# Attention and two dense stages on one core: batches one by one, the first weights kept in SBUF, W13 first, and a front in a fixed order on every engine

## The chip, the cores and the metric

The kernel runs on one core of one Trainium2 chip. The metric is the device time of one execution in microseconds (us). Matrix products run on TensorE (PE in the profile; PEld is its weight load), elementwise work on VectorE (DVE), ScalarE (ACT) and GpSimd (POOL). SyncE (SP) issues nearly all transfers.

## What is computed

```
pp  = softmax(scale * p k^T) v            # p: 32 packed queries a head; 8 batches, 8 heads, 576 keys, 64 wide
x   = softmax(scale * q pp^T) pp          # 576 queries a batch, over the 32 packed rows
x2  = ((x w1) * (x w2)) w3 w_out          # 4608 tokens, 512 -> 1024 -> 1024 -> 512
out = leaky(x2 w_in) w_out2               # 512 -> 2048 -> 512, leaky is max(0.01 h, h)
```

The inputs q, k, v and p are float32. The six weights are 64-bit floats, read as pairs of 32-bit words and turned into float32 on the chip.

## The kernel before

**The two phases.** Phase A makes x2, batch by batch, and stores it in HBM (`x2d`). Phase B makes the last line of the reference from it with a seven-product scheme (`sevens`, `h_unit`, `o_unit`). The diff changes how phase A is ordered; of phase B only where its preparation is called.

**The products.** An fp32 operand is split into a rounded high part and the rest (`hi` by ACT, `lo` by a subtraction on DVE or POOL), and `three` makes each product in three passes: hi hi, hi lo, lo hi. A pass loads 128x128 weights and streams the columns of one tile. The small attention products and M run in plain float32 on parts of the array, in bundles of eight matmuls (`eights`).

**A batch of phase A.** `s1` (scores of p on k), `e` (exp), `n` (sum and reciprocal), `t` (transposes), `y` (times v) give the packed rows `ppT`. `S`, `E`, `N`, `X` give the attention weights AT, split in two. Since x is AT times the packed rows, the kernel multiplies the packed rows by w1|w2 first: M = ppT (w1|w2), eight units `m_mm`/`m_split` of 256 columns for each of the two halves of the heads. Then a = M1 AT and b = M2 AT: 16 units of 12 passes of 288 columns (`ab_unit`), each of which copies a on ACT, multiplies it with b on DVE (line 463) and splits the product. Last, x2 is (a*b) W13 with W13 = w3 w_out, 8 units of 24 passes (`x2_unit`). W13 itself is made once, in 384 passes of 256 columns (`w13_half`).

**The order.** Batches go in pairs. For a pair all ab units come first (`ab_stage`), then all x2 units (`x2_stage`), with the attention of the next pair spread beside them. One set of split ab tiles fits in SBUF, so the second batch's a*b (and part of batch 0's) is stored to HBM (`abd`, line 96) and read back (`reload_ab`). The converted w1|w2 is stored too (`w12d`), and read back for each later pair (`load_w`). The front, a written `SCRIPT`, holds the attention of batches 0 to 3, the ab units of batches 0 and 1, and W13 at its end. The instructions are emitted in that order, and the framework's scheduler may still move them on each engine.

**A conversion of a weight block** (128x512 pairs, 512 KB): ACT makes the low word (line 296), DVE the high bits in two instructions (lines 298 and 302), POOL adds the two (line 305). There are 16 blocks of w3, 8 of w_out and 16 of w1|w2 in the front, and 32 of phase B's weights later (`pump`). For W13 the word is also split: `hi` on ACT, `lo` on DVE or POOL.

Of the kernel before, what the change touches and what calls it, by code (L numbers as in the profile page):

```python
# [10 lines left out]
SCRIPT = """k0 p0 k1 lw0 v0 s0 v1 cw0 e0 q0 n0 s1 q1 t0 e1 lw1 n1 y0 t1 p1 k2 dw0 y1 S0 cw1 k3 v2 E0 S1 s2 v3 dw1 lw2 N0 E1 e2 q2 X0 N1 n2 s3 t2 q3 X1 e3 cw2 lw3 n3 y2 t3 dw2 M00 lw4 a00 y3 S2 cw3 lw5 S3 dw3 Z M01 a01 A000 E2 cw4 lw6 A001 dw4 cw5 E3 dw5 M02 a02 A100 N2 lw7 A101 cw6 x2 M10 a10 A200 N3 dw6 cw7 A201 x3 lw8 dw7 M03 a03 A010 cw8 lw9 A011 dw8 lo0 M11 a11 A300 cw9 lw10 A301 dw9 co0 M04 a04 A110 cw10 lw11 A111 dw10 do0 M12 a12 A400 cw11 lw12 A401 dw11 lo1 O0 M05 a05 A210 cw12 lw13 A211 dw12 co1 M13 a13 A500 cw13 lw14 A501 dw13 lo2 do1 M06 a06 A310 cw14 lw15 A311 dw14 O1 co2 M14 a14 A600 cw15 lo3 A601 dw15 do2 co3 M07 a07 A410 O2 lo4 do3 A411 co4 lo5 M15 a15 A700 O3 l30 do4 A701 co5 lo6 c30 M16 a16 A510 o4 l31 do5 d30 A511 co6 c31 o5 M17 a17 A610 p2 lo7 do6 d31 A611 o6 l33 co7 l35 A710 H0 h1 do7 c33 p3 A711 o7 k4 d33 c35 l32 H3 d35 l37 c32 H5 d32 l34 c37 H2 k5 d37 c34 l38 k6 l315 d34 H4 h7 s4 c38 d38 W00 l36 c36 l39 l310 d36 h6 c39 l311 H8 e4 l312 W01 t4 W10 W20 s5 c311 v4 k7 d39 l313 d311 c310 c312 e5 c313 d310 h9 W30 v5 d312 H11 W21 h10 s6 l314 W11 n4 c314 d313 d314 q4 v7 W31 y4 t5 W40 s7 H12 q5 W41 h13 W50 n5 e6 v6 c315 d315 n6 H14 t6 W51 y5 e7 H15 y6 W60 n7 W61 W70 W71"""  # L11
KQ = {"k": 1}
# [15 lines left out]

# [4 lines left out]
def tile_kernel(ctx, tc, qT, kT, vL, pT, w12, w3b, wo1, win, wo2, out):  # L33
# [29 lines left out]
    def ps_pv():
        return ps_tile([P, 512], "pv", 2) if psum["early"] else ps_at()[:, 0]
# [5 lines left out]

    stA = ExitStack()
    main = stA.enter_context(tc.tile_pool(name="main", bufs=1, side="right"))
    stT = ExitStack()
# [3 lines left out]
    w12d = dram.tile([16, P, 512], F32, name="w12d")  # L79
    wid = dram.tile([16, P, 512], F32, name="wid")  # L80
    wod = dram.tile([16, P, 512], F32, name="wod")
    abd = dram.tile([B, 8, P, S], F32, name="abd")
    pks = [att.tile([P, 4, 32], F32, name=f"pks{i}") for i in range(2)]
    ppT = [att.tile([P, 4, 32], F32, name=f"ppT{i}") for i in range(4)]

    later = []
    RAW, VB, C64, C32, WSP, AB32, CT = 4, 5, 3, 6, 4, 7, 5

    def store(out, in_):

        later.append((out, in_))

    def stores(keep=0):
        while len(later) > keep:
            o, i = later.pop(0)
            nc.scalar.dma_start(out=o, in_=i)
# [8 lines left out]
    fence, float32s = [], []  # L105

    def together(ins, begin=False):

        if begin:
            del float32s[:]  # L110
        if float32s:
            after(ins, float32s[-1])
        else:
            tc.keep_in_program_order(ins)
        float32s.append(ins)
        fence[:] = [ins]

    def three(dst, lhs, rhs, first=True, last=True):

        for n, (i, j) in enumerate(PASSES):  # L120
            ins = nc.tensor.matmul(dst, lhs(i), rhs(j), start=first and n == 0, stop=last and n == 2)  # L121
            if fence:
                after(ins, fence.pop())
# [5 lines left out]
    s1q, s2q = {}, {}  # L129
    raws, vs, s1p, Ps, PTs, s2p, ATs = {}, {}, {}, {}, {}, {}, {}  # L130

    def half_tile(th):
        return main.tile([P, 2, TH], F32R, tag=f"ab{th}", name="ab", bufs=8)

    kq_tag = dict(KQ)

    def held(b, ins):

        if b in (2, 3):
            tc.keep_in_program_order(ins)  # L140

    def load_kq(key, b, g):
        for j in range(2):
            if key in kq_tag and b < 2:
                t = rd(half_tile(kq_tag[key])).rearrange("p a s -> p (a s)")
            else:
                t = att.tile([P, S], F32, tag="raw", name="raw", bufs=RAW)
            held(b, nc.sync.dma_start(out=t, in_=(kT if key == "k" else qT)[b, 2 * g + j]))
            raws[key, b, g, j] = t

    def spare_v(b, g):

        if (b, g) != (0, 1):
            return None
        t = main.tile([P, 2, S], F32, tag="AT", name="v", bufs=4)
        return t.rearrange("p a s -> p (a s)")[:, :5 * P].rearrange("p (c d) -> p c d", c=5)

    def load_v(b, g):
        for j in range(2):
            t = spare_v(b, g) if psum["early"] else None  # L160
            if t is None:
                t = att.tile([P, 5, P], F32, tag="v", name="v", bufs=VB)
            src = vL[b, 2 * g + j]
            held(b, nc.sync.dma_start(out=t[:, 0:4], in_=src[0:512].rearrange("(p c) d -> p c d", c=4)))
# [45 lines left out]
    def s1_norm(b, g):  # L210
        _, st = s1p[b, g]
# [41 lines left out]
    def s2_mm(b, g):
        if g == 0:
            s2q[b] = scores(ppT[b % 4], "q", b, b)
        ps = s2q[b][g]
        t = att.tile([P, 18, 32], F32, tag="sT", name="sT", bufs=2)
        nc.vector.transpose(out=t.rearrange("p (a n) c -> p a (n c)", a=2), in_=ps[:, :, :TH])
# [3 lines left out]
        s2p[b, g] = t, st  # L262

    def s2_exp(b, g):
        t, _ = s2p[b, g]
        nc.scalar.activation(out=t, in_=t, func=AF.Exp, scale=SCALE)

    def s2_norm(b, g):
        t, st = s2p[b, g]
# [6 lines left out]
        s2p[b, g] = a32  # L276

    def s2_split(b, g, engine=nc.vector):
        a32 = s2p.pop((b, g))
        at = main.tile([P, 2, S], F32R, tag="AT", name="AT", bufs=4)  # L280
        nc.scalar.copy(at[:, 0], a32)
        sub(engine, at[:, 1], a32, at[:, 0])
        ATs[b, g] = at


    def conv(dst, d, in_turn=lambda ins: None):
# [3 lines left out]

        hw, lw = d[:, :, 1], d[:, :, 0]
        q = dst.bitcast(I32)
        t = att.tile([P, 512], U32, tag="cT", name="cT", bufs=CT)
        in_turn(nc.scalar.activation(out=q, in_=lw, func=AF.Copy, scale=2.0 ** -29))
        in_turn(
            nc.vector.tensor_scalar(  # L298
# [730 lines left out]
```

## Time and profile before

| what | value |
|---|---|
| median of 3 runs | 1357.84 us (1357.84 to 1358.12) |
| profiled execution, its own time | 1356.27 us |
| its span, first to last instruction | 1354.3 us |
| PE busy | 1286.0 us, 95% |
| DVE, ACT, POOL busy | 894.1 us (66%), 629.3 us (46%), 115.7 us (9%) |
| moved by DMA | 323.62 MB |
| DMA issues to and from `abd` | 80 and 80, 144 KB each |
| DMA issues to and from `w12d` | 16 of 256 KB and 24 of 512 KB |

The profiled execution took 1.97 us more than its span, and the median is 1.57 us above it. A busy PE is not a PE at its peak, so the passes are counted in the rows below, and not its share alone.

### The profile page before, as it was taken

How to read it: one execution, taken by the hardware profiler on the slowest of the kernel's cores; microseconds unless marked ns; L12 is line 12 of the kernel's file. 1: busy time of each engine (PE TensorE's matmuls, PEld its weight loads, DVE VectorE, ACT ScalarE, POOL GpSimd, SP SyncE). 2: the span in 40 equal slices, each digit the busy share in tenths (PEclk: the TensorE clock that was granted, in tenths of full speed). 3: DMA queues.
4: the chain of work that ended last, by engine and by line, in shares of the span. 5: the costliest groups of instructions: out<-in, count | busy, mean ns of one | idle time of the engine just before them, and what ended most of it. 6: DMA issues, size and time to landing. Idle time of an engine off the chain costs nothing.

```text
span 1354.3 us, 25514 instructions
## 1 busy us (share of the span) xinstructions
PE 1286.0 (95%) x9752; PEld 1207.4 (89%) x9752; DVE 894.1 (66%) x1514; ACT 629.3 (46%) x1213; POOL 115.7 (9%) x94
## 2 busy tenths in 40 slices
PE   4587899999999999999999999999999999999998
PEld 1476798989988897899999999999999999999998
DVE  3869647765876595572977665847665468596667
ACT  2445344454455544453665555545434344354432
POOL 1245421211001200000000000000000000000000
PEclk9999999999999999999999999999999999999999
DMA  9578769768986873297878976467546754778884
GB/s 319 175 235 267 262 200 286 240 215 267 316 282 213 279 249 124 71 310 250 300 267 291 316 262 234 163 215 246 185 142 214 235 184 167 258 272 305 281 307 152
DMA packets 171258, 323.62 MB, mean 239 GB/s; under 512 B 18048, under 2 KB 89728, under 8 KB 171136
## 3 DMA queue, kind: packets, MB, share of 16 engines
q1 hardware_dynamic: 150400, 300.74, 66.1%
q10 hardware_dynamic: 20736, 21.24, 4.6%
q8 instruction: 77, 1.26, 0.4%
q14 instruction: 45, 0.37, 0.1%
HBM read 226.75 MB, written 95.16 MB: 238 GB/s over the span
## 4 chain that ended last, share of the span: by engine, by line
PE 77%; DMA 12%; DVE 7%; issue 2%; ACT 1%; SPq 1%; ACTq 0%; POOL 0%; DVEq 0%; POOLq 0%
PE mm L121 26%; PE b L884 26%; PE c L884 13%; PE a L884 6%; PE at L177 3%; DMA xh<-xfd 3%; DMA c<-w 2%; DMA xl<-xfd 1%; DVE cT L298 1%; DMA part<-o 1%; DVE cT L302 1%; DMA c<-w3b 1%; PE at L238 1%; DMA v<-vL 1%; DMA wi<-wid 1%
## 5 line engine op out<-in xcount | busy, mean ns | idle before, releaser
L121 PEld LDWEIGHTS mm<-AT,M 128*128 128x128 f32 x1536 | 210.8, 191 | 44.8 <-issue 17.1
L121 PE MATMUL mm<-AT,M 128*128 128x288 f32 x1536 | 231.2, 304 | 15.2 <-DVE ab L463 8.9
L884 PE MATMUL b<-xh,wi 128*128 128x384 f32 x768 | 219.0, 338 | 5.7 <-DMA xh<-xfd 3.7
L884 PE MATMUL b<-gh,wo 128*128 128x384 f32 x768 | 213.9, 335 | 1.4 <-DVE o L847 1.4
L121 PE MATMUL mm<-ab,W 128*128 128x288 f32 x1536 | 208.0, 295 | 0.0
L121 PEld LDWEIGHTS mm<-ab,W 128*128 128x128 f32 x1536 | 203.7, 188 | 4.5 <-issue 1.8
L884 PEld LDWEIGHTS b<-xh,wi 128*128 128x128 f32 x768 | 141.5, 189 | 8.0 <-DMA xh<-xfd 2.9
L884 PEld LDWEIGHTS b<-gh,wo 128*128 128x128 f32 x768 | 140.2, 188 | 2.3 <-issue 1.0
L884 PE MATMUL b<-xl,wi 128*128 128x384 f32 x384 | 129.2, 337 | 0.1
L884 PE MATMUL b<-gl,wo 128*128 128x384 f32 x384 | 128.4, 334 | 0.0
L884 PE MATMUL c<-xh,wi 128*128 128x384 f32 x384 | 106.1, 335 | 1.9 <-DMA xh<-xfd 1.9
L884 PE MATMUL c<-gh,wo 128*128 128x384 f32 x384 | 107.2, 335 | 0.6 <-DVE o L842 0.5
L658 ACT CAST gh<-gr 128x1152 fp32r<-128x1152 f32 (+1 forms) x72 | 75.6, 1051 | 68.8 <-PE b L884 32.5
L126 DVE TENSOR_TENSOR gl<-gr,gh 128x1152 fp32r<-128x1152 f32 (+1 forms) x72 | 87.7, 1223 | 23.9 <-ACT gh L658 23.9
L305 POOL TENSOR_TENSOR c<-cT,c 128x512 int32<-128x512 int32 x56 | 76.0, 1358 | 301.6 <-DVE cT L302 102.6
L126 DVE TENSOR_TENSOR ab<-ab,ab 128x288 fp32r<-128x288 f32 x128 | 57.8, 479 | 46.6 <-ACT ab L442 46.2
L658 ACT CAST gh<-gs 128x1152 fp32r<-128x1152 f32 (+1 forms) x54 | 56.9, 1054 | 64.0 <-PE b L884 34.8
L463 DVE TENSOR_TENSOR ab<-mm,a 128x288 f32<-128x288 f32 x128 | 57.8, 454 | 36.3 <-PE mm L121 24.6
L832 ACT ACTIVATE gr<-gr 128x1152 f32<-128x1152 f32 (+1 forms) x54 | 57.3, 1062 | 46.2 <-DVE gr L847 45.9
L884 PEld LDWEIGHTS b<-xl,wi 128*128 128x128 f32 x384 | 72.6, 189 | 0.7 <-DMA xl<-xfd 0.7
L884 PEld LDWEIGHTS c<-xh,wi 128*128 128x128 f32 x384 | 69.9, 188 | 2.9 <-DMA xh<-xfd 2.0
L884 PEld LDWEIGHTS b<-gl,wo 128*128 128x128 f32 x384 | 72.1, 188 | 0.2 <-DVE gl L126 0.2
(135 smaller groups left out, 2092.2 us busy)
## 6 DMA issues: line engine op xcount, KB each, us to landing
xh<-xfd SPq DMA_DIRECT2D x126, 384.0 KB, 5.7
xl<-xfd SPq DMA_DIRECT2D x126, 384.0 KB, 5.4
part<-o SPq DMA_DIRECT2D x48, 384.0 KB, 2.8
o<-part SPq DMA_DIRECT2D x48, 384.0 KB, 4.0
c<-wo SPq DMA_DIRECT2D x24, 512.0 KB, 4.6
w<-w12d SPq DMA_DIRECT2D x24, 512.0 KB, 4.2
abd<-ab ACTq DMA_DIRECT2D x80, 144.0 KB, 3.5
ab<-abd SPq DMA_DIRECT2D x80, 144.0 KB, 4.1
```

Source lines behind the costliest of these rows:

```text
L121: ins = nc.tensor.matmul(dst, lhs(i), rhs(j), start=first and n == 0, stop=last and n == 2)
L126: engine.tensor_tensor(out=out, in0=x, in1=rd(hi), op=ALU.subtract)
L177: ins = nc.tensor.matmul(dst(h)[c * 32:c * 32 + 32], lhs[r, c, :], rhs(c)[r], start=True, stop=True)
L238: ins = nc.tensor.matmul(ps[r, :64], PT[:K, c, r], v[:K, c, g * 64:g * 64 + 64], start=c == 0, stop=c == 4)
L298: nc.vector.tensor_scalar(out=t, in0=hw, scalar1=3, scalar2=0x3FFFFFFF, op0=ALU.logical_shift_left, op1=ALU.bitwise_and)
L302: nc.vector.scalar_tensor_tensor(out=t, in0=hw, scalar=0xC0000000, in1=t, op0=ALU.bitwise_and, op1=ALU.bitwise_or)
L305: return lambda: nc.gpsimd.tensor_tensor(out=q, in0=t.bitcast(I32), in1=q, op=ALU.add)
L463: nc.vector.tensor_tensor(out=t, in0=pb[:, :TH], in1=a, op=ALU.mult)
L658: nc.scalar.copy(hi[step], x[step])
L832: nc.scalar.activation(out=out, in_=x, func=AF.Prelu, alpha=0.01)
L884: nc.tensor.matmul(dst, lhs(l), rhs(r), start=first and n == 0, stop=last and n == total - 1, skip_group_check=True)
```

## The change

- One batch after the other: 16 ab units, then the 8 x2 units, with the attention of the next batch spread beside them (`pieces`, `slots`, `attention`). a*b is never stored. `abd` and `w12d` are gone.
- w1|w2 stays in SBUF as float32 in four tiles of 2048 columns (`ring`), in the buffers that the split w3 used before. M is made in four units of 512 columns a batch instead of eight of 256, in two PSUM banks each; its tiles have two buffers instead of three.
- W13 is made first, in 192 passes of 512 columns, with four accumulation banks open at a time. The front holds attention and all other work of batch 0, and attention of batch 1.
- The front's steps are finer (one engine each), and `manual_schedule` keeps every engine in the script's order.
- Seven buffers take weight blocks in the front (three, and four halves of the unused M tiles). The loop converts phase B's blocks as before.
- Phase B's preparation (`make_wi(0)`) comes 9 units into the last batch, 15 units ahead of phase A's end.

In the new script `l` loads a block, `c` makes the low word (ACT), `b` the bits (DVE), `j` adds (POOL), `h` is the high part (ACT), `r` and `r'` the low part on DVE and POOL, `w.fc.jc` three passes of W13, `wh` and `wl` its evacuation (ACT and DVE); `M`, `A`, `U` are the units of M, ab and x2.

```diff
+SCRIPT = """
+l.3.0 l.o.1 l.3.2 l.o.2 l.o.0 k.0.1 p.0 l.3.4 l.o.3 k.0.0 c.3.0 b.3.0 v.0.0 c.o.1 b.o.1 j.3.0 l.3.6 v.0.1 h.3.0 b.3.2
...
+l.w.2 wh.1 j.3.11 h.3.10 N.0.0 l.w.3 s.1 r'.3.10 h.3.11 c.3.15 q.1.0 r'.3.11 q.1.1 b.3.15 X.0.0 j.3.12 c.3.13 b.3.13
+c.3.14 j.3.15 h.3.12 b.3.14 l.w.4 r'.3.12 h.3.15 b.w.1 l.w.5 j.3.13 l.w.6 j.3.14 wl.0 h.3.13 b.w.2 w.4.0 r'.3.13
+h.3.14 w.4.1 w.4.2 b.w.3 r'.3.14 w.4.3 w.4.4 wl.2 r'.3.15 w.4.6 wl.3 w.4.7 wl.1 x'.0.0 w.4.5 m.1.0 w.5.0 c.w.1 m.1.1
...
+w.7.2 wl.4 j.w.6 l.w.9 M.0.0 c.w.7 b.w.7 w.7.3 Mh.0.0 b.w.8 w.7.4 j.w.7 l.w.10 w.7.5 w.7.6 Ml.0.0 w.7.7 b.w.9 w.6.7
+wh.7 w.6.5 M.0.1 b.w.10 c.w.8 c.w.9 j.w.8 l.w.11 t.1.0 Mh.0.1 wl.5 l.w.14 j.w.9 wl.7 A.0.0.0 c.w.10 Ml.0.1 wh.6 l.w.13
...
+    def ring(store, i):
+        if i not in store:
+            store[i] = wts.tile([P, 4, 512], F32, tag="w", name="w", bufs=4)
+        return store[i]
...
+    def conv_word(key, i):
+        words[key, i] = ring(w12_of, i // 4)[:, i % 4] if key == "w" else word_tile()
+        word(words[key, i], read[key, i])
...
+    def w13_mm(fc, jc):
+        if fc not in w13p:
+            w13p[fc] = ps_mm()
...
+        three(
+            w13p[fc], lambda i: w[:, 2 * h + i, c:c + P], lambda i: o_of[jc][i], n == 1, n == 8
         )
...
+    def m_mm(b, f):
+        ps = ps_at()
+        w = w12_of[f]
+        eights(lambda h: ps[:, h], ppT[b % 2], lambda c: w[:, c])
...
+    AB = [(2 * f + n, th) for f in range(4) for th in range(2) for n in range(2)]
+    X2 = [(th, e) for th in range(2) for e in range(4)]
...
+    def attention(b):
+
+        d = {s: [] for s in range(24)}
...
+        d[16] += [lambda: s2_mm(b)]
...
+        d[21] += [lambda: m_unit(b, 0)]
...
+    def rest_of_m(b):
+        return {4 * f - 4: [lambda f=f: m_unit(b, f)] for f in range(1, 4)}
...
+    scripted[0] = True
+    with tc.manual_schedule():
+        for x in SCRIPT.split():
...
+    PUMPS = (0, 6, 6, 6, 5, 5, 4)
...
+        slots(enumerate(pieces(b)), rest_of_m(b), attention(b + 1), pumps(PUMPS[b]), staging)
...
+    slots(last[:9], rest_of_m(7))
...
+    fill = {9: [lambda: make_wi(0)], 10: [lambda: load_forms(0, ORDER[:4])]}
+    slots(last, fill, spread(stage_b(2, 1), 11, 23))
```

## Rows read from the trace of the kernel before

**Rows 1.** Windows by stage: width, busy us of each engine, clock, DMA share, GB/s

```profile
0.00:58.37 58.37, 24.36 (x343) 12.13 (x343) 32.08 (x62) 18.54 (x39) 14.25 (x17) 1.00 0.80 276
58.37:140.25 81.88, 70.40 (x615) 57.55 (x608) 68.36 (x111) 41.62 (x91) 39.20 (x32) 0.98 0.71 230
253.90:380.46 126.56, 126.47 (x1336) 112.87 (x1335) 84.56 (x173) 62.11 (x148) 15.54 (x12) 1.00 0.81 263
380.46:509.32 128.86, 127.86 (x1336) 112.88 (x1335) 89.12 (x180) 64.27 (x153) 16.34 (x12) 1.00 0.79 254
509.32:631.86 122.54, 119.40 (x1050) 109.60 (x1050) 63.69 (x128) 53.40 (x128) 0.00 (x0) 0.99 0.54 177
631.86:1354.30 722.44, 708.56 (x4034) 701.02 (x4032) 483.59 (x723) 337.93 (x535) 0.00 (x0) 1.00 0.69 239
```

**Rows 2.** PE's waits, 0 to 200 us, then the longest of 200 to 632

```profile
PE mm L121 <- DVE ab L463: 7.8, 11, 1.6
...
PE mm L121 <- ACT M L429: 2.2, 2, 1.9
```

**Rows 3.** Timeline of PE: start, us, line, tiles, count

```profile
233.51 1.20 PE L177 MATMUL at<-raw,ppT 64*32 64x288 f32 x32
234.64 19.33 PE L121 MATMUL mm<-ab,W 128*128 128x288 f32 x144
...
261.83 0.66 PE L177 MATMUL at<-w,ppT 64*32 64x256 f32 x16
262.42 1.86 PE L121 MATMUL mm<-AT,M 128*128 128x288 f32 x12
264.21 0.66 PE L177 MATMUL at<-w,ppT 64*32 64x256 f32 x16
...
581.30 50.71 PE L121 MATMUL mm<-ab,W 128*128 128x288 f32 x384
```

**Rows 4.** Timeline of DVE and POOL around 122 us, and one of POOL later

```profile
121.40 0.68 DVE L302 SCALAR_TENSOR_TENSOR cT<-c,cT 128x512 uint32<-128x512 uint32 x1
...
122.00 0.41 DVE L298 TENSOR_SCALAR cT<-c 128x512 uint32<-128x512 uint32 x1
...
122.25 1.31 POOL L305 TENSOR_TENSOR c<-cT,c 128x512 int32<-128x512 int32 x1 [2.09 <-DVE cT L302]
122.33 0.68 DVE L126 TENSOR_TENSOR M<-at,M 128x512 fp32r<-128x512 f32 x1
...
122.93 1.18 DVE L302 SCALAR_TENSOR_TENSOR cT<-c,cT 128x512 uint32<-128x512 uint32 x1
...
123.52 1.76 POOL L126 TENSOR_TENSOR wsp<-c,wsp 128x512 fp32r<-128x512 f32 x1
...
156.86 1.30 POOL L126 TENSOR_TENSOR wsp<-c,wsp 128x512 fp32r<-128x512 f32 x1
```

**Rows 5.** Groups of POOL and DVE by line, 103.7 to 140 us

```profile
L305 POOL TENSOR_TENSOR c<-cT,c 128x512 int32<-128x512 int32 x13 | 17.8, 1366 | 17.1 <-DVE cT L302 14.4 <-ACT a L461 1.6 <-DVE ab L463 1.0
L126 POOL TENSOR_TENSOR ab<-c,ab 128x256 fp32r<-128x256 f32 x2 | 2.1, 1046 | 0.0
L126 POOL TENSOR_TENSOR wsp<-c,wsp 128x512 fp32r<-128x512 f32 x1 | 1.8, 1758 | 0.0
...
L298 DVE TENSOR_SCALAR cT<-c 128x512 uint32<-128x512 uint32 x12 | 11.8, 981 | 0.0
L302 DVE SCALAR_TENSOR_TENSOR cT<-c,cT 128x512 uint32<-128x512 uint32 x12 | 9.5, 793 | 0.0
L126 DVE TENSOR_TENSOR ab<-c,ab 128x256 fp32r<-128x256 f32 x8 | 5.8, 744 | 0.0
...
L126 DVE TENSOR_TENSOR wsp<-c,wsp 128x512 fp32r<-128x512 f32 x3 | 3.1, 1048 | 0.0
```

**Rows 6.** The first weight block: its issue on SP, its first use on DVE

```profile
3.06 0.43 SPq L314 DMA_DIRECT2D c<-w  x1
...
8.63 0.43 DVE L298 TENSOR_SCALAR cT<-c 128x512 uint32<-128x512 uint32 x1 [8.63 <-DMA c<-w]
```

More of the change, by code (lines that the diff above doesn't have):

```diff
@@ L78, in tile_kernel @@
     W13 = main.tile([P, 8, 2, DM], F32R, name="W13")
[L79 to L82, printed above, removed]
+    ppT = [wts.tile([P, 4, 32], F32, name=f"ppT{i}") for i in range(2)]
     pks = [att.tile([P, 4, 32], F32, name=f"pks{i}") for i in range(2)]
[L84 to L96, printed above, removed]
+    RAW, VB, C64, C32, CT = 4, 5, 3, 4, 3
+    scripted = [False]
+    fence, float32s = [], []
     def after(ins, other):
@@ L326, in conv_end, with join @@
-    def conv_end(key, i):
-        add, t = begun.pop((key, i))
-        add()
-        if key == "w":
-            nc.sync.dma_start(out=w12d[i], in_=t)
-        half[key, i] = t
+        return t
+    def join(out, t):
+        q = out.bitcast(I32)
+        nc.gpsimd.tensor_tensor(out=q, in0=t.bitcast(I32), in1=q, op=ALU.add)
+    sources = {"o": wo1, "3": w3b, "w": w12}
+    read, words, tbits, split, spare, loads = {}, {}, {}, {}, [], [0]
+    o_of, w3_of, w12_of = {}, {}, {}
+    def ring(store, i):
+        if i not in store:
+            store[i] = wts.tile([P, 4, 512], F32, tag="w", name="w", bufs=4)
+        return store[i]
@@ new lines, in conv_load @@
+    def conv_load(key, i):
+        n = 0
+        if key != "w" or i < 4:
+            n = loads[0] % (C64 + 4)
+            loads[0] += 1
+        if n < C64:
+            t = att.tile([P, 512, 2], U32, tag="c64", name="c64", bufs=C64)
+        else:
+            if (n - C64) % 2 == 0:
+                spare[:] = [main.tile([P, 2, 2, 512], F32R, tag="M", name="M", bufs=2).bitcast(U32)]
+            m = spare[0][:, (n - C64) % 2]
+            t = m.rearrange("p a c -> p (a c)").rearrange("p (n w) -> p n w", w=2)
+        nc.sync.dma_start(out=t, in_=sources[key][i])
+        read[key, i] = t
@@ L333, in word_tile, with conv_bits, conv_join @@
     def word_tile():
         return att.tile([P, 512], F32, tag="c32", name="c32", bufs=C32)
-    def conv_push(key, src, n, dst=None):
-        conv_todo.extend((key, src, i, dst) for i in range(n))
-        conv_load()
-    def conv_load():
+    def conv_word(key, i):
+        words[key, i] = ring(w12_of, i // 4)[:, i % 4] if key == "w" else word_tile()
+        word(words[key, i], read[key, i])
+    def conv_bits(key, i):
+        tbits[key, i] = bits(read[key, i])
+    def conv_join(key, i):
+        join(words[key, i], tbits.pop((key, i)))
@@ new lines, in conv_hi, with conv_lo @@
+    def conv_hi(key, i):
+        if key == "o":
+            o_of[i] = [half_tile(k).rearrange("p a s -> p (a s)")[:, :512] for k in range(2)]
+            split[key, i] = o_of[i]
+        else:
+            t = ring(w3_of, i // 2).bitcast(F32R)
+            split[key, i] = [t[:, 2 * (i % 2) + k] for k in range(2)]
+        nc.scalar.copy(split[key, i][0], words[key, i])
+    def conv_lo(key, i, engine=nc.vector):
+        hi, lo = split.pop((key, i))
+        sub(engine, lo, words.pop((key, i)), hi)
@@ L341, in conv_load, with conv_push, conv_fetch @@
+    conv_todo, conv_in, conv_open, conv_out = [], [], [], []
+    def conv_push(src, n, dst):
+        conv_todo.extend((src[i], dst[i]) for i in range(n))
+    def conv_fetch():
         while conv_todo and len(conv_in) < C64 - 1:
-            key, src, i, dst = conv_todo.pop(0)
+            src, dst = conv_todo.pop(0)
             d = att.tile([P, 512, 2], U32, tag="c64", name="c64", bufs=C64)
-            nc.sync.dma_start(out=d, in_=src[i])
-            conv_in.append((key, d, i, dst))
-    def conv_close():
-        while conv_open:
-            _, (add, out, t) = conv_open.popitem()
-            add()
-            if out is not None:
-                conv_out.append((out, t))
@@ L354, in pump @@
-    def pump(n=1):
-        for _ in range(n):
-            while conv_out:
-                o, t = conv_out.pop(0)
-                nc.sync.dma_start(out=o, in_=t)
-            if not conv_in:
-                conv_close()
-                return
-            key, d, i, dst = conv_in.pop(0)
-            conv_load()
-            if key == "w":
-                if i % 2 == 0:
-                    pair["w"] = att.tile([P, 2, 512], F32, tag="wsp", name="w32", bufs=WSP)
-                t = pair["w"][:, i % 2]
-            else:
-                t = word_tile()
-            add = conv(t, d, tc.keep_in_program_order)
-            conv_close()
-            half[key, i] = t
-            conv_open[key, i] = add, None if dst is None else dst[i], t
@@ new lines, in conv_fetch, with pump, conv_flush @@
+            conv_in.append((d, dst))
+    def pump():
+        conv_flush()
+        if not conv_in:
+            return
+        d, dst = conv_in.pop(0)
+        conv_fetch()
+        t = word_tile()
+        tc.keep_in_program_order(nc.scalar.activation(out=t.bitcast(I32), in_=d[:, :, 0], func=AF.Copy, scale=2.0 ** -29))
+        u = bits(d, tc.keep_in_program_order)
+        conv_open.append((t, u, dst))
+    def conv_flush():
+        for t, dst in conv_out:
+            nc.sync.dma_start(out=dst, in_=t)
+        del conv_out[:]
+        for t, u, dst in conv_open:
+            join(t, u)
+            conv_out.append((t, dst))
+        del conv_open[:]
@@ new lines, in ab_mm, with ab_a @@
+    def ab_mm(b, fc, th):
+        m = Mt[b, fc // 2]
+        pair = ps_mm(), ps_mm()
+        for w in range(2):
+            c = fc % 2 * 256 + w * P
+            for g in range(2):
+                at = ATs[b, g]
+                three(
+                    pair[w][:, :TH], lambda i: m[:, i, g, c:c + P], lambda i: at[:, i, th * TH:(th + 1) * TH],
+                    g == 0, g == 1,
+                )
+        abp[fc, th] = pair
+    def ab_a(fc, th):
+        pa, pb = abp[fc, th]
+        a = main.tile([P, TH], F32, tag="a", name="a", bufs=2)
+        nc.scalar.copy(a, pa[:, :TH])
+        abp[fc, th] = a, pb
@@ new lines, in tile_kernel, with pumps @@
+    conv_push(wo2, 16, wod)
+    conv_fetch()
+    def pumps(n, first=7):
+        d = {}
+        for s in (5, 10, 14, 18, 20, 22)[:n]:
+            d[s] = [pump]
+            d[s + 1] = [conv_flush]
+        return d
+    PUMPS = (0, 6, 6, 6, 5, 5, 4)
+    STAGE = {2: (0, 0), 3: (0, 1), 4: (1, 0), 5: (1, 1), 6: (2, 0)}
+    for b in range(1, 7):
+        staging = spread(stage_att(*STAGE[b]), 16, 23) if b in STAGE else {}
+        slots(enumerate(pieces(b)), rest_of_m(b), attention(b + 1), pumps(PUMPS[b]), staging)
```

567 lines of the change are left out of this document (197 added, 370 removed).

## The prediction

> **What bounds the kernel now.** I read the stage windows first, then PE's waits, then PE's timeline. The windows [rows 1] show phase B, 722.44 us from 631.86 on, with 4034 passes in 708.56 busy us: PE streams without gaps, 0.176 us a pass of 384 columns. Phase A's middle, 253.90 to 509.32, is as full: two pairs of batches, 126.56 and 128.86 us. The holes are in front: 24.36 busy us in the first 58.37, and 70.40 in the next 81.88, in which PE does the 384 ab passes of batches 0 and 1. The waits [rows 2] say what is late there: DVE's a*b (11 waits, 7.8 us, the longest of PE's waits on passes). From 200 to 632 us the longest wait is 2.2 us and none is on a DMA, although DMA is busy 0.79 to 0.81 of the middle. So PE bounds the loop, and the conversions bound the front.
>
> PE's timeline [rows 3] prices the work. The 384 passes from 581.30 to 631.86 take 50.56 us: 0.132 us a pass of 288 columns. A unit of M issued at 261.83 is followed 2.38 us later by the next, with 12 passes (1.58 us) between: 0.80 us a unit, 0.59 of it up to the first pass (261.83 to 262.42), and 0.21 that the passes behind it lose at the switch. Two bundles of 288 columns take 1.13 us (233.51 to 234.64).
>
> **The spills.** 160 transfers of 144 KB and 40 of w1|w2 go. They cost PE nothing now, since none of its waits past 200 us is on them [rows 2]; I give them nothing. If DMA had bound the middle, this would be the whole gain. The batch-wise order itself moves work and adds none: the same 384 passes of 288 columns a batch.
>
> **M in 512 columns.** From 256 columns (0.59) to 2 x 288 (1.13) is 0.54 us for 320 columns, 1.7 ns a column. A unit of 512 takes 0.59 + 256 x 0.0017 = 1.02, with the switch 1.23 us. A batch pays 4 x 1.23 = 4.9 instead of 8 x 0.80 = 6.4: 1.5 us less. Bounds: 0 (twice the unit) and 3.2 (columns free). I take 1.5, since the columns have a slope in the rows.
>
> **A batch in the new loop.** The two middle pairs give (126.56 + 128.86) / 4 = 63.9 us a batch, attention of the next included; less 1.5 is 62.4. The last, without attention, is 122.54 / 2 - 1.5 = 59.8. From the first unit of M of batch 0 to phase A's end: 7 x 62.4 + 59.8 = 496.6 us.
>
> New waits in the loop: M now fills a whole pair of PSUM banks, of which there are two pairs, and is emptied by one ACT and one DVE instruction of double size. Attention's bundles queue behind M on PE for these pairs. Three ab units, 4.7 us, lie between M and the next user, and the emptying should take about twice the 0.68 us of DVE's half (the 122.33 instruction [rows 4]) and as much on ACT, 2.5 to 3 us. I take 0, with 2 us a batch as the upper bound.
>
> **The front.** Here the order of work decides. PE does W13 (64 units of three 512-column passes; from 0.132 at 288 and 0.176 at 384 columns a pass is 0.23, a unit 0.70 us, 45 us in all) and batch 0's attention, and waits for weights most of the time. Two things gate it. First, four banks are open for fc 0 to 3; `w.4.0` needs `wl.0` on DVE, which stands in DVE's fixed order behind 25 pairs of bit instructions. After it PE has 32 units, 22 us, and two of M. Second, unit `M.0.2` needs `j.w.8` to `11`, the 33rd to 36th addition on POOL, and their words take the buffer of w3's fc 6, so they also wait for W13's end. What POOL does is therefore what PE waits for.
>
> The timeline around 122 us shows how DVE and POOL share [rows 4]. POOL's addition starts at 122.25 and ends at 123.56; DVE's second bit instruction, issued at 122.93, takes 1.18 us instead of the 0.60 from its start to the next one's at 121.40. It ends at 124.11, and POOL's subtraction, issued at 123.52, takes 1.76 instead of the 1.30 at 156.86. Each waited until the other was done. So their times add up. Alone they hold: addition 1.27 (122.25 to 123.52), POOL subtraction 1.30, DVE bits 0.33 + 0.60 (122.00 to 122.33, 121.40 to 122.00), DVE subtraction of 512 columns about 0.60, as the second bit instruction.
>
> The Trainium skill states this outright: SBUF — State Buffer, section "SBUF: two separate sides", calls the port pair of VectorE and GpSimd an exclusive lock that one instruction holds to its end while the other fully blocks, for DVE instructions with two SBUF inputs or in a two-port mode. The trace agrees (1.18 for 0.60, 1.76 for 1.30). By that rule the two columns below are added; without it POOL's alone would count.
>
> Up to `j.w.11` the script has on POOL 36 additions (45.7 us), 21 subtractions `r'` (27.3) and one of 576 columns (1.5): 74.5 us. On DVE it has 36 pairs of bits (33.5), three subtractions (1.8), and four softmax instructions and one subtraction of batch 0 (3.4, by columns): 38.7 us. Together 113.2.
>
> How full can they be? From 103.7 to 140 us [rows 5] there are 13 additions, 2 half and one whole subtraction on POOL (16.5 + 1.3 + 1.3) and 12 pairs of bits, 8 half and 3 whole subtractions on DVE (11.2 + 2.6 + 1.8): 34.7 of 36.3 us, 0.96. The new order is fixed and waits now and then for ACT and PE, so I take 0.92, between 0.98 and 0.80. The first block was issued at 3.06 and used 5.6 us later [rows 6], behind 1.2 MB; the new script issues it first: use at about 5 us. `M.0.2` then starts at F = 5 + 113.2 / 0.92 = 128 us (120.5 at 0.98, 146.5 at 0.80). The other gate gives less: up to `wl.0` 22 additions, 17 subtractions and 27 us of DVE are 77 us, 5 + 77 / 0.92 = 89; with 22 us of W13, 2.5 of M and four additions beside DVE's bits (about 9) M.0.2 comes at 122.
>
> Before M.0.2 PE has already done two units of M (2.5), four ab units (48 passes, 6.3), and of batch 1's attention the scores and one transpose (1.9): 10.7 us of the 496.6. Left: 485.9. The other 12 ab units run beside DVE's softmax of batch 1; 3 us for that (0 to 8).
>
> **Sum.** Phase A ends at 128 + 485.9 + 3 = 617 us, against 631.86: 15 us less. Phase B is unchanged, 722.4: its preparation comes 36 us (7 x 1.58 + 8 x 3.17) ahead of phase A's end, enough for some 15 us of DVE work beside x2. Span 1339.5; with the 1.97 outside it 1341.4; the median lies 1.57 higher: 1343 us. In other words, the front stays as hollow as it was, and the gain is what M saves (12 us) and what DVE no longer holds up.
>
> **The rivals.** Less than 0.2% (2.7 us) can't be told from no change here.
>
> *As forecast*, the shared port sets the front: 1343, its own range 1325 to 1354 (F from 120.5 to 138, the 0 to 8 us, half of M's upper bound). Chance 0.67.
>
> *POOL and DVE overlap after all*, so that POOL's 74.5 us alone counts: `wl.0` at 57, W13 done at 82, M.0.2 at 90; 38 us earlier, 1305. Rows 4 speak against it [rows 4]; for it, DVE may slip in where POOL waits. Chance 0.08.
>
> *The loop waits for PSUM.* At 2 us for each of 7 batches the gain is gone: 1357. For it: two pairs for M, scores and transposes, and M's waits are the longest of the middle already [rows 2]. Against it: three units of cover. Chance 0.08.
>
> *The fixed order stalls the front: slower.* In a queue that cannot be reordered one late step holds all behind it: DVE waits in order for batch 0's scores, exp and transposes from PE and ACT, the bits wait behind, POOL starves, `wl.0` comes late and with it the second half of W13. Price: one for one. It decides from F = 143 on, a share of 0.82; at 0.78 F is 150 and the time 1365. For it: the order was laid down ahead with durations that need not be these, and DVE's first bit instruction takes 0.41 us alone and 0.98 on the mean beside POOL [rows 4, 5]. Against it: seven buffers of loads, and the front before, in which the scheduler chose, kept PE busy for no more than 0.86 of its second stretch [rows 1]. Chance 0.17.
>
> **The numbers.** Faster: 0.67 + 0.08 + 0.02 of the PSUM case = 0.77. Same: the other 0.06 of that case, and 0.02 of the stalls, with F near 143. Slower: the 0.15 of the stalls that is left. The range leaves out the overlap case and the far end of the stalls: 1315 to 1361.
>
> **What would show it.** M.0.2 (the third bundle of 512 columns) between 120 and 138 us; POOL and DVE instructions longer than alone all through the first 100 us; PE full from there to the end of phase A, which comes near 617; M units followed after 1.0 us by passes; 62 to 63 us a batch; no spill transfers and no gain from them; phase B 722 us. It would be wrong if POOL idles long in the first 100 us, if bundles in the loop wait for ACT's or DVE's emptying of M, or if phase B's first passes wait for its weights.

## The result, and the profile after

The changed kernel takes 1335.73 us in the median (1334.15 to 1337.1, four runs) beside 1357.98 for the kernel before on the same chip: a ratio of 0.9831 (0.9814 to 0.9848), 22 us less. The profiled execution took 1334.15 us, its span is 1332.4. The forecast was 1343 in a range of 1315 to 1361. One repeat of the changed kernel had an execution of 4331.66 us, in which nearly all of PE's passes took more than twice as long for no reason that its trace shows; the ratio of that repeat leaves it out.

The windows of the changed kernel (columns as in [rows 1]) are cut at 57.34, where the last passes of W13's first half begin, at W13's second half (80.42), at the third bundle of M (`M.0.2`, 124.86), at the first bundles of M inside batches 1, 2, 3 and 7, and at phase B.

```profile
0.00:57.34 57.34, 31.23 (x231) 19.80 (x232) 50.22 (x51) 26.38 (x48) 44.07 (x36) 0.93 0.91 332
57.34:80.42 23.08, 8.35 (x53) 5.91 (x53) 22.64 (x24) 11.68 (x20) 20.20 (x14) 0.65 0.62 212
80.42:124.86 44.44, 38.91 (x266) 30.33 (x267) 43.55 (x57) 19.38 (x39) 27.50 (x21) 0.90 0.44 142
124.86:175.99 51.13, 51.13 (x430) 47.32 (x430) 25.21 (x45) 19.26 (x44) 4.27 (x5) 1.00 0.21 70
...
237.68:299.35 61.67, 61.67 (x605) 55.38 (x604) 43.76 (x85) 31.34 (x72) 7.75 (x6) 1.00 0.62 202
546.85:604.33 57.48, 54.36 (x421) 50.13 (x420) 26.50 (x57) 21.88 (x53) 0.00 (x0) 1.00 0.40 142
604.33:1332.40 728.07, 709.26 (x4032) 701.12 (x4032) 482.80 (x722) 336.32 (x532) 0.00 (x0) 1.00 0.69 235
```

Phase A ends at 604.33 instead of 631.86, 27.5 us earlier. From `M.0.2` to batch 7 PE has next to no hole: 51.13 busy of 51.13, then 61.67 of 61.67. A middle batch takes 61.67 us, where the pairs gave 63.9. The front is as hollow as it was, but shorter: 46.4 us of holes in 124.86, where the kernel before had 45.5 in its first 140.25. In it DVE is busy 50.22 + 22.64 + 43.55 = 116.4 us, which includes what its instructions wait. Phase B gives 5.6 us back: 728.07 instead of 722.44, for the same work. All in all DMA moves 283.10 MB instead of 323.62.

PE's waits, 0 to 200 us and then 200 to 604:

```profile
PE mm L120 <- DVE W L125: 17.0, 2, 14.7
PE mm L120 <- ACT ab L328: 11.3, 3, 10.1
PE mm L120 <- DVE ab L125: 8.9, 2, 4.8
PE mm L120 <- POOL ab L125: 5.9, 3, 3.3
...
PE mm L120 <- ACT a L428: 1.7, 1, 1.7
PE mm L120 <- DVE ab L434: 0.8, 2, 0.5
```

All long waits lie in the front, mostly for splits of weight blocks and of W13. In the loop 2.5 us are left, none of them for M. PE's timeline shows the front's gates and, at the end, a unit of M in the loop:

```profile
57.34 7.22 PE L120 MATMUL mm<-ab,w 128*128 128x512 f32 x20 [4.75 <-DVE ab L125]
64.49 1.20 PE L153 MATMUL at<-raw,pks 64*32 64x288 f32 x32
80.42 20.03 PE L120 MATMUL mm<-ab,w 128*128 128x512 f32 x75 [14.73 <-DVE W L125]
100.38 1.09 PE L153 MATMUL at<-w,ppT 64*32 64x512 f32 x16
101.40 5.07 PE L120 MATMUL mm<-ab,w 128*128 128x512 f32 x21
106.40 1.09 PE L153 MATMUL at<-w,ppT 64*32 64x512 f32 x16
...
118.85 3.45 PE L120 MATMUL mm<-AT,M 128*128 128x288 f32 x24
124.86 1.09 PE L153 MATMUL at<-w,ppT 64*32 64x512 f32 x16 [2.56 <-issue]
...
228.53 1.09 PE L153 MATMUL at<-w,ppT 64*32 64x512 f32 x16
229.55 6.62 PE L120 MATMUL mm<-ab,W 128*128 128x288 f32 x48
```

The 14.73 us ahead of 80.42 are the wait for `wl.0`. A unit of M takes 1.02 us to the first pass behind it (228.53 to 229.55), the 1.02 that the forecast had worked out.

DVE, and then POOL, between 33 and 38 us show how the two share (start, us; compare [rows 4]):

```profile
33.08 0.41 DVE L269 TENSOR_SCALAR cT<-M 128x512 uint32<-128x512 uint32 x1
33.53 1.67 DVE L272 SCALAR_TENSOR_TENSOR cT<-M,cT 128x512 uint32<-128x512 uint32 x1
35.11 0.42 DVE L269 TENSOR_SCALAR cT<-M 128x512 uint32<-128x512 uint32 x1
35.57 1.66 DVE L272 SCALAR_TENSOR_TENSOR cT<-M,cT 128x512 uint32<-128x512 uint32 x1
```

```profile
33.30 1.34 POOL L279 TENSOR_TENSOR c<-cT,c 128x512 int32<-128x512 int32 x1 [0.69 <-ACT w L328]
35.34 1.33 POOL L279 TENSOR_TENSOR c<-cT,c 128x512 int32<-128x512 int32 x1 [0.70 <-ACT ab L328]
```

The addition starts at 33.30, while DVE's first bit instruction (33.08 to 33.49) still runs. The second one, 0.69 us where POOL is idle, takes 1.67: it ends 0.6 us after the addition. One block costs 2.04 us (33.30 to 35.34), not the 0.33 + 0.60 + 1.27 = 2.20 of the forecast's columns. Where POOL also has a subtraction for each block, the first bit instruction waits too: 1.49 us at 43.93, beside a subtraction that runs from 43.42 to 45.14 on POOL's timeline:

```profile
43.93 1.49 DVE L269 TENSOR_SCALAR cT<-c 128x512 uint32<-128x512 uint32 x1
45.45 1.66 DVE L272 SCALAR_TENSOR_TENSOR cT<-c,cT 128x512 uint32<-128x512 uint32 x1
47.04 1.49 DVE L269 TENSOR_SCALAR cT<-c 128x512 uint32<-128x512 uint32 x1
```

Such a block costs 3.11 us (43.93 to 47.04), where the columns have 2.20 + 1.30 = 3.50.

### The profile page after: what moved, and what is told of

It is laid out like the page before. It is cut to its first block, busy times and chain, and to the rows that moved or that the text cites. A ratio compares the mean times of both kernels' runs of the same rounds, so it can differ in the third digit from the quotient of the medians.

```text
span 1332.4 us, 23526 instructions
## 1 busy us (share of the span) xinstructions
PE 1264.0 (95%) x9048; PEld 1187.1 (89%) x9048; DVE 908.5 (68%) x1455; ACT 623.9 (47%) x1165; POOL 138.6 (10%) x105
## 2 busy tenths in 40 slices
DMA packets 139377, 283.10 MB, mean 212 GB/s; under 512 B 14849, under 2 KB 66049, under 8 KB 139265
## 4 chain that ended last, share of the span: by engine, by line
PE 74%; DMA 11%; DVE 8%; issue 3%; POOL 1%; SPq 1%; ACT 1%; POOLq 0%; ACTq 0%; DVEq 0%
PE mm L120 26%; PE b L750 25%; PE c L750 13%; PE a L750 6%; DMA xh<-xfd 4%; PE at L153 3%; DVE cT L269 2%; DMA xl<-xfd 1%; DVE cT L272 1%; DMA part<-o 1%; DMA wi<-wid 1%; PE at L211 1%; DMA xfd<-P 1%; POOL c L279 1%; DMA v<-vL 1%
## 5 line engine op out<-in xcount | busy, mean ns | idle before, releaser
L120 PEld LDWEIGHTS mm<-AT,M 128*128 128x128 f32 x1536 | 207.1, 188 | 31.4 <-issue 10.7
L120 PE MATMUL mm<-AT,M 128*128 128x288 f32 x1536 | 223.2, 300 | 5.0 <-DVE W L125 2.3
L540 ACT CAST gh<-gr 128x1152 fp32r<-128x1152 f32 (+1 forms) x72 | 75.7, 1052 | 69.1 <-PE b L750 32.2
L125 DVE TENSOR_TENSOR gl<-gr,gh 128x1152 fp32r<-128x1152 f32 (+1 forms) x72 | 87.7, 1223 | 23.4 <-ACT gh L540 23.3
L120 PE MATMUL mm<-ab,w 128*128 128x512 f32 x192 | 57.1, 454 | 40.8 <-DVE W L125 14.7
L120 PEld LDWEIGHTS mm<-ab,w 128*128 128x128 f32 x192 | 41.0, 220 | 56.1 <-DVE W L125 15.3
L125 DVE TENSOR_TENSOR ab<-ab,ab 128x288 fp32r<-128x288 f32 x124 | 61.3, 496 | 35.5 <-ACT ab L439 33.7
L439 ACT CAST ab<-ab 128x288 fp32r<-128x288 f32 x128 | 55.1, 432 | 45.3 <-DVE ab L434 45.1
```

The costliest lines, as they stand in the source:

```text
L125: engine.tensor_tensor(out=out, in0=x, in1=rd(hi), op=ALU.subtract)
L439: nc.scalar.copy(t[:, 0], ab32[fc, th])
L540: nc.scalar.copy(hi[step], x[step])
```

## The experiments

Every median stands beside the kernel before on the same chip; the ratio is to that.

**The changed kernel and the kernel before, once more.**

> The changed kernel itself, beside the other kernels of this call on the same chip. Expected: the time within 3 us of 1335.7; M.0.2 near 124.9 and phase A's end near 604.3 us, and phase B again some 728 us against 722.4 in the kernel before, if that difference belongs to the change; nearer 722 if it was chance.

Measured: 1336.35 us in the median of five, 0.9805 (0.9773 to 0.9838). The landmarks were not read a second time, as its one trace is of the execution that the ratio leaves out.

> The kernel before once more, for a second length of its phase B. If the changed kernel's longer phase B (728.1 against 722.4 us) belongs to the change, this gives 721 to 724; if such lengths vary from run to run, it lies as often near 727.

Measured: one time, 1362.42 us; phase A 636.50 (631.86 in the first trace), phase B 723.9.

**One bit instruction instead of two in the front.** The high words of the 40 front conversions then lack their top two bits, so the output is not the reference's; what is timed is DVE's second instruction (0.6 us of port each), while POOL does as much as before.

```diff
-        nc.vector.scalar_tensor_tensor(
+        if not scripted[0]:
+            nc.vector.scalar_tensor_tensor(
```

> Leaves out the second bit instruction of the 40 conversions in the front (sign and top bit of the exponent are lost); POOL's work is untouched. Theory (port times add up): 0.60 us less for each, so 25 x 0.60 = 15 us before wl.0, near 65 instead of 79.7, and up to 22 us before the 36th addition; M.0.2 near 105 to 110. Rival 1 (POOL's own work sets the front): wl.0 within 3 us of 79.7. Rival 2 (fixed order with waits for ACT and PE): a few us, under 6. POOL's additions should then take 1.3 us each instead of 1.4 and its subtractions 1.3 instead of 1.7.

Measured: one time, 1308.97 us. `wl.0` starts at 62.86 instead of 79.68, `M.0.2` at 101.56 instead of 124.86, phase A ends at 579.99.

```profile
62.86 0.68 DVE L125 TENSOR_TENSOR W<-mm,W 128x512 fp32r<-128x512 f32 x1
```

```profile
101.56 1.09 PE L153 MATMUL at<-w,ppT 64*32 64x512 f32 x16 [1.95 <-issue]
```

The 40 instructions are 24 us alone, and 23.3 us came off `M.0.2`. POOL's queue was not touched, so the rival in which POOL's own work sets the front falls. These 24 us of DVE's work count in full. One part of the expectation missed: POOL's additions did not fall to 1.3 us (1.42 and 1.38 on the mean of the two groups, 1.44 and 1.37 in the changed kernel), and its subtractions only to 1.40 and 1.48, from 1.68 and 1.58. DVE's first bit instruction is still there beside them.

**The front's `r'` subtractions on DVE.**

```diff
-        "r'": lambda key, i: conv_lo(key, i, nc.gpsimd),
+        "r'": lambda key, i: conv_lo(key, i, nc.vector),
```

> The 21 low parts r' of the front go from POOL to DVE, at the same places of the fixed order. Landmarks in the changed kernel: the first W13 evacuation on DVE (wl.0) starts at 79.7 us, the unit M.0.2 at 124.9, phase A ends at 604.3. Theory (DVE's and POOL's port times add up): a subtraction holds the port 0.60 us on DVE and 1.30 on POOL, so 17 x 0.70 = 12 us come off before wl.0 (near 67 us) and 15 us before the 36th addition; phase A ends some 8 to 15 us earlier, near 592, the time near 1324. Rival 1 (POOL's own work counts, DVE overlaps): POOL loses 17 x 1.3 = 22 us before wl.0, which comes near 57. Rival 2 (the fixed order waits for ACT and PE rather than for the port): wl.0 stays within 3 us, or comes later, since DVE now waits in order for POOL's additions and ACT's high parts; the time stays or rises.

Measured: 1332.68 us, 0.981 (0.9772 to 0.9849). `wl.0` starts at 75.7, not 67, and `M.0.2` at 120.9; phase A ends at 604.49, as before the edit, since the 4 us are lost again in the loop (batches of 61.7 to 64.2). The theory's direction was right, its size was not: `M.0.2` came 4.0 us earlier, where the sum of the two engines' work fell by 15.

**The front without a fixed order** (the scheduler may move instructions).

```diff
-    with tc.manual_schedule():
-        for x in SCRIPT.split():
+    for x in SCRIPT.split():
```

> The same script, but the framework's scheduler may move the front's instructions on each engine as it may in the kernel before. Theory (the port's sum sets the front, 113 us of work): the order changes little of the sum, M.0.2 stays between 115 and 140, the time within 10 us of 1335. Rival 1 (the fixed order is where the gain is): the front gets longer by 10 us or more, 1345 to 1360. Rival 2 (the fixed order costs): DVE's n.1 and wl steps move up, M.0.2 before 115, the time near 1325.

Measured: 1330.7 us, 0.9795 (0.9736 to 0.9855). `wl.0` starts at 64.69, 15 us earlier, yet `M.0.2` at 122.84 and phase A ends at 604.86. The fixed order neither makes the gain nor costs anything that can be told.

**Another order on DVE**: `wl.0` to `wl.3` directly behind their `wh`, `n.1` behind `e.1`.

```diff
-w.2.7 D.0.1 l.w.0 wh.0 w.3.4 c.3.11 r'.3.8 w.3.5 h.3.9 w.3.6 wh.2 r'.3.9 b.3.11 w.3.7 c.3.12 E.0.1 j.3.10 wh.3 b.3.12
+w.2.7 D.0.1 l.w.0 wh.0 wl.0 w.3.4 c.3.11 r'.3.8 w.3.5 h.3.9 w.3.6 wh.2 wl.2 r'.3.9 b.3.11 w.3.7 c.3.12 E.0.1 j.3.10
...
-Aa.0.1 Aa.1.1 Al.1.0 j.w.15 n.1.0 n.1.1 Y.1.0 Am.0.1 Y.1.1 M.0.2 Am.1.1 Ah.0.1 Ah.1.1 Al.0.1 A.0.2.0 Al.1.1 Mh.0.2
+j.w.12 Aa.0.1 Aa.1.1 Al.1.0 j.w.15 Y.1.0 Am.0.1 Y.1.1 M.0.2 Am.1.1 Ah.0.1 Ah.1.1 Al.0.1 A.0.2.0 Al.1.1 Mh.0.2 Ml.0.2
```

> Six steps of the fixed order move on DVE: the evacuations wl.0, wl.2, wl.3, wl.1 come directly behind their wh, and n.1.0, n.1.1 directly behind e.1.0, e.1.1. No work is added or taken away. Theory (DVE's queue holds the free banks and the scales back behind the bits, which wait for the port): wl.0 at 60 to 66 us instead of 79.7, PE begins the second half of W13 there and ends it near 92 instead of 106; M.0.2 then waits for the 36th addition, near 113 to 118 instead of 124.9; phase A ends 7 to 12 us earlier, the time near 1326. Rival (the port's sum alone sets M.0.2): W13 ends earlier, but M.0.2 and the time move by less than 3 us. Rival 2 (DVE waits at the new places for ACT's wh, and the bits behind it come late): M.0.2 later.

Measured: 1333.76 us, 0.9793 (0.9762 to 0.9823). `wl.0` at 63.65, but W13 done at 105.3 (106.5 in the changed kernel), the first ab pass at 108.60 and `M.0.2` at 123.77. W13's wait for `wl.0` goes, and PE, on which `M.0.0` stands ahead of W13's last 21 passes, waits 7.0 us for the additions of w1|w2 instead: 16 us won at one gate are 1 us at the next. That is the first rival.

**Both, that order and `r'` on DVE.**

> The six moved steps and the 21 low parts on DVE together. Port work up to the 36th addition falls from 113 to 98 us. Theory (the port's sum gates the first ab unit, as the two runs with only one of these changes suggest): the first ab pass at 95 to 100 us instead of 108, phase A's end 6 to 10 us earlier, the time near 1327. Rival (DVE, in a fixed order, now waits for POOL's additions and ACT's high parts before each low part): first ab pass later than 103, the time within 3 us of 1333.

Measured: 1330.14 us, 0.9772 (0.9737 to 0.9807). First ab pass at 105.11, `M.0.2` at 119.78, phase A ends at 601.52. By first pass and time this is the rival, although `M.0.2` comes 4.0 us earlier than by that order alone.

**No fixed order, and `r'` on DVE.**

> The 21 low parts on DVE, and the scheduler free to move the front's instructions. Theory (port sum 98 instead of 113 us, and no queue held by a fixed order): first ab pass 8 to 12 us earlier than in the free order alone, phase A's end near 594, the time near 1322. Rival (the scheduler does not place the instructions by the port): first ab pass and time as in the free order alone, 1327 to 1334.

Measured: 1328.52 us (1323.72 to 1331.16), 0.977 (0.9744 to 0.9796): the fastest that computes the reference, although its interval overlaps the one before it and that of the changed kernel's repeat. `M.0.2` at 118.89, 4.0 us earlier than in the free order alone; phase A ends at 598.76, not near 594; phase B takes 730.6. The time lies in the rival's range.

**M in halves of 256 columns again**, in the loop alone, one slot apart.

```diff
-    def m_unit(b, f):
-        m_mm(b, f)
+    def m_half(b, f, k):
+        c = slice(k * 256, k * 256 + 256)
...
+        eights(lambda h: ps[:, h, :256], ppT[b % 2], lambda i: w[:, i, c])
```

> M of the loop's batches is made in halves of 256 columns again, each with its own bundle and evacuation, one slot apart; the front is as in the changed kernel. Theory (M in 512 columns gives 1.5 us a batch: 1.23 a unit against 2 x 0.80): a batch goes from 61.7 to 63.2, seven batches 10 us, phase A's end near 614, the time near 1346. Rival (the batch gained 2.2 us from the order by single batches, not from M): a batch stays within 0.4 us of 61.7, the time within 3 us of 1335.7.

Measured: 1342.38 us, 0.9884 (0.9844 to 0.9924). Phase A ends at 613.88, 9.55 later, and a batch without any hole takes 62.92:

```profile
273.68:336.60 62.92, 62.92 (x670) 56.18 (x668) 43.35 (x89) 32.20 (x76) 8.17 (x6) 1.00 0.65 207
```

So M in 512 columns is worth 62.92 - 61.67 = 1.25 us a batch.

**The spills put back**: in batches 1 to 7 every a*b is stored (112 stores on ACT's queue), and as many blocks are loaded on SP, into a tile that nothing reads.

```diff
+        nc.scalar.dma_start(out=abd[b, fc, :, th * TH:(th + 1) * TH], in_=ab32[fc, th])
...
+            t = main.tile([P, TH], F32, tag="back", name="back", bufs=2)
+            nc.sync.dma_start(out=t, in_=abd[b, fc, :, th * TH:(th + 1) * TH])
```

> Brings traffic back that the change took away, with nothing waiting for it: in batches 1 to 7 each of the 16 products a*b is also stored to HBM (ACT's queue) and each is read back into a spare tile beside the x2 units (SP's queue), 112 stores and 112 loads of 144 KB, more than the 80 and 80 before. Theory (DMA never bound the loop; the spills cost PE nothing): a batch stays within 0.4 us of 61.7 and the time within 3 us of the changed kernel. Rival (the transfers and their issue on ACT's queue delay a*b or the loads of the next batch): 1 to 2 us a batch, 8 to 15 us in all.

Measured: 1362.58 us, 1.0015 (0.9996 to 1.0034). Phase A ends at 633.14 and batches 2 to 5 take 67.7 to 69.0, each from its first x2 pass to the next batch's. The gain is gone; the theory missed, and the rival was too small.

**The same with seven buffers of `ab32` instead of three.**

> As the run with the spill traffic, but the products a*b have seven buffers, as in the kernel before, instead of three. With three, 1.58 us a unit gives a product 4.7 us before its buffer is wanted again, and a store lands some 3.5 us after an issue that itself waits on ACT's queue. Theory (what cost 28 us of phase A there was the wait for the buffer, not the traffic): a batch falls from 68 back to 62 to 63 us, the time within 5 us of 1336. Rival (the traffic itself, or its 16 issues a batch on ACT's queue, holds up ACT's copies and DVE's products): a batch stays above 65 us and the time above 1350.

Measured: 1360.56 us, 1.0004 (0.9984 to 1.0025); batches of 67.8 to 69.7. The buffers were not the cause. The windows of two of its batches, then PE's waits from 150 to 600:

```profile
273.57:343.29 69.72, 65.36 (x604) 57.32 (x603) 45.37 (x87) 31.93 (x74) 8.00 (x6) 0.95 0.80 257
411.62:480.01 68.39, 63.43 (x604) 55.66 (x603) 43.35 (x85) 30.44 (x72) 6.54 (x5) 1.00 0.78 248
```

```profile
PE mm L121 <- ACT M L403: 8.6, 4, 2.9
PE mm L121 <- DVE ab L435: 4.4, 6, 1.7
PE mm L121 <- DVE M L126: 2.6, 4, 0.7
PE at L154 <- DVE M L126: 2.1, 2, 1.0
```

Of the 8.1 us that the first of them takes longer than 61.67, 4.4 are holes (69.72 - 65.36) and 3.7 are more busy time, at a granted clock of 0.95. In the second, at a clock of 1.00, 5.0 are holes and 1.8 more busy time. The largest waits are for ACT's copy of M, 8.6 us of the 26. ACT's timeline, of this kernel and then of the changed one, shows such a copy coming late:

```profile
292.38 0.39 ACT L456 COPY x2s<-mm 128x288 f32<-128x288 f32 x1
296.17 0.33 ACTq L457 DMA_DIRECT2D x2d<-x2s  x1
296.54 0.66 ACT L356 ACTIVATE c<-c 128x512 int32<-128x512 uint32 x1 [3.77 <-DMA wid<-c]
...
299.90 0.33 ACTq L457 DMA_DIRECT2D x2d<-x2s  x1
300.27 1.01 ACT L403 CAST M<-at 128x1024 fp32r<-128x1024 f32 x1 [1.90 <-DMA v<-vL]
```

```profile
293.63 0.39 ACT L455 COPY x2s<-mm 128x288 f32<-128x288 f32 x1
294.05 0.33 ACTq L456 DMA_DIRECT2D x2d<-x2s  x1
294.42 1.02 ACT L402 CAST M<-at 128x1024 fp32r<-128x1024 f32 x1 [0.40 <-ACT x2s L455]
```

With the traffic, an x2 store is issued 3.4 us after its copy ended (292.77 to 296.17), and ACT, which works in order, starts the next instruction only behind it. In the changed kernel this one is issued at once (294.02 to 294.05). Not every one is, but from 140 to 600 us these gaps add up to 14 us there (62 stores that the timeline tells apart, the median 0.03) and to 53 us with the traffic (56 stores, the median 0.40). What the issue waits for the profile does not name; the releasers in brackets are inferred.

**The loads a batch later**, from a tensor for each batch and into eight buffers:

```diff
-            nc.sync.dma_start(out=t, in_=abd[b, fc, :, th * TH:(th + 1) * TH])
+            nc.sync.dma_start(out=t, in_=abd[max(b - 1, 1)][fc, :, th * TH:(th + 1) * TH])
```

> The same stores and as many loads as with seven buffers of ab32, but from batch 2 on each load reads the halves that the batch before stored (long landed), from a tensor of its own, into 8 tiles instead of 2. Theory A, that the traffic was dear since SP, which issues in order, stood at its loads (91.7 us in 31 waits for stores of ab to land, 250 to 560 us) with the loads of v, k and q behind them: batches 2 to 6 fall from 68 back to 62 to 63.5 us, the matmuls' wait for ACT's M goes, phase A ends near 606 to 612, time 1336 to 1345 us. Theory B, that the bytes themselves are dear (250 instead of 199 GB/s, loads of kT 5.7 instead of 5.1 us to landing, ACT standing at its stores): batches stay at 67 to 69 us, time 1357 to 1364.

Measured: 1360.89 us, 1.001 (0.9981 to 1.0038); batches still take 66.8 to 70.1, by their first x2 passes. But SP still stood 89.4 us in 30 waits at these loads, put down to the stores, though the data had landed a batch before. The time lies in theory B's range, but the edit did not take the wait away, so the run decides nothing between theory A and B. What the wait is for, and how the 26 us divide between SP's order and the bytes, stays open.

## Why the prediction was right, and where it was not

The span came out 7.1 us below the forecast's 1339.5. By the forecast's own parts: -3.1 at `M.0.2` (124.86 for 128), -9.5 from there to phase A's end (479.5 for 489), +5.6 in phase B.

**The shared port holds up the front.** Shown: the 24 us of DVE's work that one run leaves out came back as 23.3 at `M.0.2`. The trace agrees with the Trainium skill (SBUF — State Buffer, section "SBUF: two separate sides"), whose lock lets one of DVE and POOL wait until the other is done: DVE's second bit instruction lasts 1.67 us beside an addition, and 0.69 without one. The two rivals in the front fell: POOL alone would have put `M.0.2` at 90, and a stall beyond 143 did not come (POOL's longest pause between 6 and 100 us was 4.1). DVE's queue alone is not the bound either: with 21 subtractions more on it `M.0.2` came earlier, not later. But the sum of times alone is no price for moving work. That move should have saved 21 x 0.70 = 15 us of the sum; it saved 4.0 us at `M.0.2` in the fixed order (124.86 to 120.91), 4.0 in the other order (123.77 to 119.78) and 4.0 in the free one (122.84 to 118.89). So the fixed order is not what withholds the rest; what does was not tried.

**The gate at `M.0.2` was named wrongly.** The forecast let it wait for the 36th addition, at 128 us. That one ended at 116.24 (start 114.92 on POOL's timeline, 1.32 us): 11.8 us early. The sum was too large: its 113.2 us do not even fit into 116.2 - 5 = 111.2. A block saves 0.16 us of it (2.04 for 2.20) without a POOL subtraction and 0.39 (3.11 for 3.50) with one. As an estimate, 36 blocks save 5.8 us by the first and 14.0 by the second; what is left fills 0.97 or 0.89 of the 111.2, so whether the share of 0.92 was right stays open. The forecast's second gate came nearer to what happened, by terms that missed both ways: `wl.0` at 79.68 for 89; W13 and two units of M in 27.1 us (80.42 to 107.5) for 24.5; and then 17.4 us to `M.0.2` where "about 9" stood. That 128 lay only 3.1 us off is therefore luck in part. At its end `M.0.2` waited for ACT, which scales `pp` behind DVE's `n.1`:

```profile
122.15 1.63 DVE L272 SCALAR_TENSOR_TENSOR cT<-c,cT 128x512 uint32<-128x512 uint32 x1
...
124.50 0.16 DVE L186 RECIPROCAL st<-st 128x1 f32<-128x1 f32 x1
```

```profile
124.45 0.56 ACT L220 ACTIVATE pp<-at,st 128x64 f32<-128x64 f32 x2 [2.45 <-DVE st L186]
```

By the code the bundle needs the pair of PSUM banks that ACT empties there; this wait was not tried by itself. The order that moves `n.1` ahead won 1 us; there the waits for the additions of w1|w2 came in its place.

**M in 512 columns.** Right: 1.25 us a batch for 1.5, and 9.55 us in all where the loop's M is undone. The unit itself was 1.02 as worked out.

**The loop.** 61.67 to 62.08 a batch for 62.4 (370.9 for 374.4 over six), 57.48 for 59.8 in the last, and none of the 3 us set aside for batch 1's softmax. The rival in which the loop waits for PSUM fell: its waits are 2.5 us in all.

**The spills.** "I give them nothing" was read from PE's waits in the paired order, and for that order it nearly holds: 63.9 - 1.25 - 61.67 leaves 1.0 us a batch for the spills and all else that the batch-wise order changed. But it doesn't hold for the new order, in which the same kind of traffic costs 6 to 8 us a batch and the whole gain. It is more than before in these transfers (112 stores and 112 loads for 80 and 80), but not in all: 316.17 MB, less than the 323.62 of the kernel before. The order and the removal belong together, and the forecast had no such term.

**Phase B was not unchanged.** PE waits longer ahead of its first group (first the changed kernel, then the kernel before):

```profile
L750 PE MATMUL b<-xh,wi 128*128 128x384 f32 x768 | 219.4, 338 | 11.3 <-DMA xh<-xfd 5.6 <-ACT gr L710 5.2 <-ACT x2s L455 0.5
```

```profile
L884 PE MATMUL b<-xh,wi 128*128 128x384 f32 x768 | 219.0, 338 | 5.7 <-DMA xh<-xfd 3.7 <-ACT gr L844 2.0
```

That names 5.6 us, not their cause: 1.9 more for the loads of xh, 3.2 more for ACT's gr, and only 0.5 ahead of phase B's first pass. Phase B took 724.8 to 730.9 in all but one variant (735.8 where the loads come a batch later), 722.4 and 723.9 in the kernel before. Its preparation was not moved by itself, so this stays open.

Of the 27.5 us in phase A, 9.6 are shown to be M's. The other 18 were not taken apart by any run. By the two traces PE's busy time in phase A fell from 577.42 to 554.72 us, 22.7 of the 27.5, and its holes from 54.4 to 49.6. So the gain is mostly less busy time and not holes that closed, although a busy PE is not a PE at its peak. W13's passes have no part in it: 192 of 512 columns are busy 57.1 us, 384 of 256 columns were 48.9. And the kernel before ended its phase A at 631.86 and 636.50 in its two traces, so some of the 18 may be scatter between executions.

## What to carry to other kernels

Where DVE and POOL both work from SBUF, add their times before you look for a gate, but do not price a move between them by that sum (4 us came of 15 here), and expect that moving one step past the gate only shows the next. Waits of the bounding engine price a transfer in the order in which they were read; if the change reorders the work as well, the same transfer needs a price in the new order.

## What was not expected of the hardware

PE stopped at 65.7 us and began again at 80.42. In the windows of 5 us its granted clock reads 0.50 late in that hole, the lower of its two levels (1.2 GHz), and for the first 5 us of passes too:

```profile
75.00:80.00 5.00, 0.00 (x0) 0.00 (x0) 4.93 (x5) 1.24 (x2) 4.37 (x4) 0.50 0.86 288
80.00:85.00 5.00, 4.58 (x11) 3.62 (x12) 4.93 (x5) 0.00 (x0) 5.00 (x4) 0.50 0.10 40
85.00:90.00 5.00, 5.00 (x21) 4.08 (x20) 4.93 (x9) 1.07 (x2) 0.89 (x2) 0.87 0.00 0
90.00:95.00 5.00, 5.00 (x24) 4.14 (x23) 4.73 (x8) 3.67 (x9) 3.98 (x3) 1.00 0.01 3
```

Eleven passes lie in the window from 80.00 and 24, with those that reach over its ends, in the one from 90.00. At full clock (47 passes in 10.81 us from 89.64 on, 0.230 each) the 75 passes from 80.42 would have taken 17.3 us instead of 20.03, so the hole cost 2.8 us beyond itself.
